# Windowed attention with a gated layer behind it: statistics of the normalisation on ScalarE, one inverse for two softmaxes, shorter scale passes, and a new table of ranks

## Chip, cores and metric

One core of one Trainium2 chip. The metric is the time of one execution in device microseconds (us); the kernel before takes 561.51 us (median of 3 runs, 561.41 to 562.19).

## What is computed

For 8 batches of 8 heads, 576 positions and 64 dimensions: attention within a band of |i - j| < 4, plus attention on means of groups of 4 positions, whose result is repeated 4 times. The sum x goes through a gated layer. The lines that the change touches are the two softmaxes and the normalisation of v:

```python
a = np.exp(s); a = a / (np.sum(a, axis=-1, keepdims=True) + 1e-09)      # both attentions
h = np.maximum(x @ w_in, 0.0)
u, v = h[..., :512], h[..., 512:]
mu = np.mean(v, axis=-1, keepdims=True)
var = np.mean((v - mu) ** 2, axis=-1, keepdims=True)
v_n = (v - mu) / np.sqrt(var + 1e-06)
v_s = np.einsum('ts,bsd->btd', w_spatial, v_n) + b_spatial[None, :, None]
return (u * v_s) @ w_out
```

## The kernel before

Everything runs on one core with five queues: PE (TensorE), DVE (VectorE), ACT (ScalarE), POOL (GpSimd) and SP (DMA issue). The function `tile_kernel` describes the work as some 1,500 pieces (`plan.op`), each with an engine, a cost in ns, the tiles that it reads and writes, and a rank. `Plan.run` then walks through time and gives each engine, among the pieces that can start within `NEAR` of the earliest, the one of lowest rank. The ranks are the table `ORDER`, found by a search, one number per piece in the order in which they are declared. The strings `ON` say, piece by piece, which engine does a step that several could do (A is ACT, D is DVE, P is POOL). So the table and the strings set the order in each queue; waits are by semaphores. Where the planner expects PE to idle in the first 110 us, it puts in dummy matmuls (`warm`, L1341).

The attention runs over 32 pairs of heads (n, four per batch; `attention`). PE makes the banded scores into a PSUM tile paa or pab (L883 mask, L890), DVE takes maxima and subtracts (L903 to L918), ACT takes exponentials (L954), DVE sums (L921) and inverts (L924, L925), DVE or POOL normalises (L958), PE transposes (L966). The attention on means goes the same way: scores L937 into two of the four PSUM tiles pma to pmd, maxima L940 to L942, exponentials with their sums on ACT (L974), inverse L978 and L979, normalisation L989 or L991, for batches from 1 on a rest in half precision (L995). Then PE multiplies by v (L1091 and L1061 or L1075) and DVE adds both results into x (L1101, L1103). In batches from 1 on, x is split into two half-precision parts (L1124, L1126).

The gated layer of a batch (`gated`) has five V pieces of up to 128 rows (PE L1160, L1164, L1169; relu on ACT L1182, L1185 or L1193), eight U pieces (L1226 or L1231, relu L1237 on ACT, with sums that bound the magnitude), eight S pieces (the spatial product, L1253 to L1256, on v normalised and split into two halves vh), and O pieces (L1290, drained by ACT L1303). For each V piece, `stats` on DVE (L1173, L1174, L1176) gives mean and scaled variance, POOL raises it to -1/2 (L1195), DVE applies both (L1179), ACT makes the high half (L1199; L1205 and L1206 for the last 64 rows), DVE or POOL the low half (L1201, L1207).

Weights come as 64-bit floats; DVE unpacks them in `low`, `body` and `sign` (L643, L654, L658), `shrink` (L648, L650) is on either engine; ACT sums magnitudes (L741, L745), and `split` makes two half-precision parts (ACT L616, DVE L619). `bound` turns sums of magnitudes into a power of two and its inverse: a transpose on PE (L586), a maximum on DVE (L589), a spread on PE (L592), and five small DVE passes in `scales` (L597 to L603).

SP issues the loads of q and k (L854), v (L792, L794), and weights (L628), and the stores (L1294, L1300); POOL issues accumulating loads of v for the group means (L780).

## Time and profile before

| | |
|---|---|
| runs | 561.41, 561.51, 562.19 us |
| profiled execution: its own time, its span | 562.08 us, 560.3 us |
| PE busy | 532.8 us, 95% |
| DVE busy | 457.3 us, 82% |
| ACT busy | 355.5 us, 63% |
| POOL busy | 147.3 us, 26% |
| granted TensorE clock, mean | 0.989 |

The span runs from the first to the last instruction; the execution's own time is 1.78 us longer. Starts are counted from the span's beginning. A line's mean duration holds neither the wait before it nor the overlap with its neighbour.

### The profile page before, as it was taken

The numbers are of one execution on the slowest core, as the hardware profiler recorded it, in microseconds if no ns is written. First come the engines' busy times: TensorE is split into PE (matmuls) and PEld (weight loads), VectorE is DVE, ScalarE is ACT, GpSimd is POOL, SyncE is SP. The second block draws the span as 40 slices with busy tenths as digits, with TensorE's granted clock in tenths as the row PEclk, the third lists the DMA queues.
The fourth block names the chain that finished last, engine by engine and source line by source line (L and its number), as shares of the span: only waits on it lengthen the run. The fifth ranks groups of instructions, "written<-read, shape, count | busy, mean of one in ns | idle before, by whom it ended". The sixth has DMA issues, their size and how long they took to land.

```text
span 560.3 us, 15981 instructions
## 1 busy us (share of the span) xinstructions
PE 532.8 (95%) x6457; PEld 357.1 (64%) x6457; DVE 457.3 (82%) x1251; ACT 355.5 (63%) x905; POOL 147.3 (26%) x173
## 2 busy tenths in 40 slices
PE   5668979999999999999999999999999999999997
PEld 3446456865777566865777656856676567856673
DVE  5799999998998699897989798997779897963450
ACT  4759669857976586556766767666546566654422
POOL 6424273102622144011500144111610031111400
PEclk9889999999999999999999999999999999999999
DMA  9997775025441345234431345243253310010002
GB/s 258 282 294 212 197 180 124 1 63 176 89 129 42 108 105 133 86 108 130 111 97 54 92 126 128 87 131 87 35 135 101 109 40 26 5 39 1 37 1 94
DMA packets 40230, 59.54 MB, mean 106 GB/s; under 512 B 4028, under 2 KB 26972, under 8 KB 40158
## 3 DMA queue, kind: packets, MB, share of 16 engines
q1 hardware_dynamic: 37854, 51.46, 30.4%
q0 software_dynamic: 2304, 7.08, 7.9%
q8 instruction: 50, 0.82, 0.6%
q14 instruction: 22, 0.18, 0.1%
HBM read 46.57 MB, written 9.44 MB: 100 GB/s over the span
## 4 chain that ended last, share of the span: by engine, by line
PE 73%; DVE 14%; DMA 6%; ACT 2%; POOL 1%; issue 1%; SPq 1%; ACTq 0%; DVEq 0%; POOLq 0%
PE pmb L1290 6%; PE pma L1253 4%; PE pmd L1253 4%; PE pma L1290 4%; PE pmc L1253 4%; PE pmd L1290 3%; PE pmd L1164 3%; PE pma L1164 3%; PE pma L1231 3%; PE pmb L1253 3%; PE pmc L1231 3%; PE pmc L1290 3%; PE pmd L1231 3%; PE pmb L1164 3%; PE pmb L1231 2%; PE pmc L1164 2%
## 5 line engine op out<-in xcount | busy, mean ns | idle before, releaser
L1253 PEld LDWEIGHTS <-vha 128*128 128x128 f16 x768 | 73.2, 98 | 19.1
L1231 PEld LDWEIGHTS <-win 128*128 128x128 f16 x672 | 65.1, 98 | 17.8 <-issue 0.2
L958 POOL TENSOR_TENSOR sb<-sb,smb 128x640 f32<-128x640 f32 x11 | 15.1, 1374 | 75.4 <-DVE smb L925 45.6
L1290 PEld LDWEIGHTS <-g 128*128 128x128 f16 x192 | 18.5, 98 | 20.8
L1290 PEld LDWEIGHTS <-more 128*128 128x128 f16 x192 | 18.3, 98 | 20.7
L1253 PE MATMUL pma<-wsp,vha 128*128 128x256 f16 (+1 forms) x216 | 28.5, 281 | 0.0
L1253 PE MATMUL pmd<-wsp,vha 128*128 128x320 f16 (+1 forms) x192 | 27.8, 294 | 0.0
L1253 PE MATMUL pmc<-wsp,vha 128*128 128x256 f16 (+1 forms) x204 | 27.0, 282 | 0.0
L1290 PE MATMUL pmb<-wo,more 128*128 128x512 f16 x96 | 22.0, 379 | 0.0
L1253 PE MATMUL pmb<-wsp,vha 128*128 128x320 f16 (+1 forms) x156 | 21.5, 287 | 0.0
L861 POOL TENSOR_TENSOR suma<-qka 128x576 f32<-128x576 f32 x9 | 10.8, 1198 | 37.3 <-DMA qka<-qk_dram 27.5
L958 POOL TENSOR_TENSOR sa<-sa,sma 128x640 f32<-128x640 f32 x8 | 11.1, 1389 | 34.5 <-DVE sma L925 23.3
L1195 POOL TENSOR_TENSOR stc<-stc,mhalf 128x1 f32<-128x1 f32 x13 | 9.0, 691 | 40.8 <-DVE stc L1176 40.8
L1195 POOL TENSOR_TENSOR sta<-sta,mhalf 128x1 f32<-128x1 f32 (+1 forms) x14 | 11.1, 792 | 32.3 <-DVE sta L1176 20.3
L1195 POOL TENSOR_TENSOR stb<-stb,mhalf 128x1 f32<-128x1 f32 (+1 forms) x13 | 9.2, 708 | 36.5 <-DVE stb L1176 32.8
L861 POOL TENSOR_TENSOR suma<-qkb 128x576 f32<-128x576 f32 x7 | 8.1, 1160 | 33.8 <-DMA qkb<-qk_dram 33.8
L780 POOL DMA_DIRECT2D tv<-v_dram x15 | 13.6, 910 | 11.7 <-DMA tv<-v_dram 10.6
L995 DVE SCALAR_TENSOR_TENSOR ehb<-edb,smdb,ehb 128x144 f16<-128x144 f32 x42 | 16.2, 450 | 0.0
L954 ACT ACTIVATE sb<-sb 128x640 f32<-128x640 f32 x16 | 11.7, 732 | 4.8 <-DVE sb L909 4.8
L954 ACT ACTIVATE sa<-sa 128x640 f32<-128x640 f32 x16 | 11.8, 736 | 4.7 <-DVE sa L918 2.6
L1164 PEld LDWEIGHTS <-xa 128*128 128x128 f16 x84 | 8.2, 98 | 9.9
L995 DVE SCALAR_TENSOR_TENSOR eha<-eda,smda,eha 128x144 f16<-128x144 f32 x42 | 14.5, 409 | 0.0
(1023 smaller groups left out, 1712.4 us busy)
## 6 DMA issues: line engine op xcount, KB each, us to landing
qka<-qk_dram SPq DMA_DIRECT2D x16, 576.0 KB
qkb<-qk_dram SPq DMA_DIRECT2D x16, 576.0 KB
tv<-v_dram POOLq DMA_DIRECT2D x15, 288.0 KB, 5.1
wst<-v_dram POOLq DMA_DIRECT2D x9, 288.0 KB, 4.6
stg<-w_in_dram SPq DMA_DIRECT2D x5, 512.0 KB
out_dram<-rowc SPq DMA_DIRECT2D x8, 256.0 KB
out_dram<-rowb SPq DMA_DIRECT2D x7, 256.0 KB
out_dram<-rowe SPq DMA_DIRECT2D x7, 256.0 KB
```

Source lines behind the costliest of these rows:

```text
L780: plan.op("POOL", 850, lambda r=r: nc.gpsimd.dma_start(t.ap, v4[b, r], accum_op=ALU.add), w=[t], rank=rank + 2.0 + 0.3 * r, kb=288, name="tv")
L861: side(s1).tensor_tensor(sb.ap.rearrange("p x (g r) -> p x g r", r=2), x[:, :, :, :2], x[:, :, :, 2:], op=ALU.add)
L954: exp_of.append(plan.op("ACT", 637, lambda: nc.scalar.activation(s.ap, s.ap, AF.Exp, scale=1.0 / 8.0), w=[s], rank=R["E"], name="exp"))
L958: plan.op(nm, 0, lambda: side(nm).tensor_tensor(s.ap, s.ap, sm.ap[:, :, None].broadcast_to([P, NW, 64]), op=ALU.mult), r=[sm], w=[s], rank ...
L995: nc.vector.scalar_tensor_tensor(eh.ap[:, a, :, 1], ed.ap[:, a, :], smd.ap[:, a:a + 1], eh.ap[:, a, :, 0], op0=ALU.mult, op1=ALU.subtract)
L1164: nc.tensor.matmul(ps.ap, xs[c].ap[:, i, t * P:(t + 1) * P], win[:, c, j, FF:], start=(c == 0 and (i, j) == (0, 0)), stop=(c == NC - 1 and ...
L1195: plan.op("POOL", 700, lambda: nc.gpsimd.tensor_tensor(st.ap[:r, 8:9], st.ap[:r, 8:9], mhalf[:r], op=ALU.pow), w=[st], rank=rank - EVICT, ...
L1231: nc.tensor.matmul(ps.ap[:, :n], win[:, c, i, ft * P:(ft + 1) * P], xs[c].ap[:, j, HA[h]:HA[h + 1]], start=(c == 0 and (i, j) == (0, 0)), ...
L1253: nc.tensor.matmul(ps.ap[:, :n], vh.ap[:, c, i, fs], wsp[:, c, j, hs], start=(c == 0 and (i, j) == (0, 0)), stop=False)
L1290: nc.tensor.matmul(ps.ap, g.ap[:, c, i, k:k + P] if t < NT else gt.ap[:, c, i], wo[:, c, j, :], start=(c == 0 and (i, j) == (0, 0)), stop= ...
```

## The change

Part 1, normalisation. Relu on ACT now also sums the row (`accum_out`). A small step `mean` makes -sum/512 on one of three engines, ACT makes a second pass (`squares`, a Square with that bias and a sum), POOL makes the scaled variance and its power -1/2 and, where needed, the product with the mean (`root`), and `apply` is on DVE or ACT. Tile st has five buffers in place of three. `stats` is gone.

```diff
-            def stats():
-                nc.vector.bn_stats(st.ap[:r, :6], vr.ap[:r])
-                nc.vector.bn_aggr(st.ap[:r, 6:8], st.ap[:r, :6])
-                nc.vector.tensor_scalar(st.ap[:r, 8:9], st.ap[:r, 7:8], 1.0e-6, 2.0**-20, op0=ALU.add, op1=ALU.mult)
+            def mean():
+                if mu.eng == "ACT":
+                    nc.scalar.mul(st.ap[:r, 1:2], st.ap[:r, :1], -1.0 / FF)
+                else:
+                    side(mu).tensor_scalar(st.ap[:r, 1:2], st.ap[:r, :1], -1.0 / FF, None, op0=ALU.mult)
+            def squares():
+                nc.scalar.activation(junk[:r, :FF], vr.ap[:r], AF.Square, bias=st.ap[:r, 1:2], accum_out=st.ap[:r, 2:3])
+            def root():
+                nc.gpsimd.tensor_scalar(st.ap[:r, 8:9], st.ap[:r, 2:3], 2.0**-20 / FF, 1.0e-6 * 2.0**-20, op0=ALU.mult, op1=ALU.add)
+                nc.gpsimd.tensor_tensor(st.ap[:r, 8:9], st.ap[:r, 8:9], mhalf[:r], op=ALU.pow)
+                if ap.eng == "ACT":
+                    nc.gpsimd.tensor_tensor(st.ap[:r, 9:10], st.ap[:r, 8:9], st.ap[:r, 1:2], op=ALU.mult)
             def apply():
-                nc.vector.tensor_scalar(vr.ap[:r], vr.ap[:r], st.ap[:r, 6:7], st.ap[:r, 8:9], op0=ALU.subtract, op1=ALU.mult)
+                if ap.eng == "ACT":
+                    nc.scalar.activation(vr.ap[:r], vr.ap[:r], AF.Identity, bias=st.ap[:r, 9:10], scale=st.ap[:r, 8:9])
+                else:
+                    nc.vector.tensor_scalar(vr.ap[:r], vr.ap[:r], st.ap[:r, 1:2], st.ap[:r, 8:9], op0=ALU.add, op1=ALU.mult)
```

Part 2, the softmaxes. The sums of both (10 and 3 columns) stand in one tile; two DVE instructions replace four. `times` holds the factors that differ.

```diff
-            nc.vector.tensor_scalar(sm.ap, sm.ap, 1.0e-9, None, op0=ALU.add)
+            nc.vector.scalar_tensor_tensor(sm.ap, sm.ap, 1.0e-9, times[:, 0 if whole else 1], op0=ALU.add, op1=ALU.mult)
             nc.vector.reciprocal(sm.ap, sm.ap)
-        def inverse_d():
-            nc.vector.tensor_scalar(smd.ap, smd.ap, 1.0e-9, 4.0 if whole else 2.0**-8, op0=ALU.add, op1=ALU.mult)
-            nc.vector.reciprocal(smd.ap, smd.ap)
```

The first eight pairs (`solo`) put the scores on means into one PSUM tile, heads side by side, so one maximum replaces two:

```diff
+            if solo:
+                nc.vector.tensor_reduce(mxd.ap, pd[0].ap[:, :3 * G].rearrange("p (a k) -> p a k", a=3), axis=AX.X, op=ALU.max)
+            else:
+                nc.vector.tensor_reduce(mxd.ap[:, :1], down(0), axis=AX.X, op=ALU.max)
...
```

Part 3, bounds. Five small passes become three; four where the bound has a factor. The floor comes from extra columns that POOL sets at the start (ten more memsets there, one of them in place of DVE's L710).

```diff
-                nc.vector.tensor_copy(t()[:, 7:8], pb.ap[:, P:P + 1])
+                nc.vector.tensor_scalar(e, pb.ap[:, P:P + 1].bitcast(I32), 0x7F800000, None, op0=ALU.bitwise_and)
...
-            nc.vector.tensor_scalar(e, e, -1.0, -low * 2.0**23, op0=ALU.mult, op1=ALU.min)
-            nc.vector.tensor_scalar_add(sc, e, (268.0 - up) * 2**23)
-            nc.vector.tensor_scalar(iv, e, -1.0, (up - 14.0 + fac) * 2**23, op0=ALU.mult, op1=ALU.add)
+            nc.vector.tensor_scalar(sc, e, -1.0, (268.0 - up) * 2**23, op0=ALU.mult, op1=ALU.add)
+            nc.vector.tensor_scalar_add(iv, e, (up - 14.0 + fac) * 2**23)
```

Part 4, the order. `ORDER` is a new table, and `ON` has new strings (two are new):

```diff
-ON = {"shrink": "ADAAAADAADAA",
+ON = {"shrink": "ADAAAAAADDAA",
+      "mean": "PDPPDDADADAPDAAAADDAPAAPDADAPDADDDAPPPD",
+      "apply": "DDDAADADAAAAADDDAADADADDAAADAAAAADDADAAA",
-      "norm": "PDPPPPPPPPDPDPDPPPDPDPPDDDDDDDPP",
-      "normd": "PDAAAAAPAAAPDADDPAAAPPDDAPPPDDPA",
-      "vlo": "PPDPDPPDDDDDDDDPDDDDPPPDDPDPDDPDDDDPDPP"}
+      "norm": "PDPPPPPDDDDDPPDPPPPDDDPDPDDDPDDP",
+      "normd": "DDAAAAAAPDADPPAPAPPAPDAAAPAPDDPD",
+      "vlo": "DDDPDDPDPDDPPDDPDPDDPDPDDDDDPDDDPDDDPPD"}
```

On DVE, in the middle of batch 0's V pieces, before: the statistics of the second piece (row tile rowe), splits of the WV weights (win), and the next statistics.

```order
L1173 BN_STATS stb<-rowe 128x6
L1174 BN_AGGR stb<-stb 128x2
L1176 TENSOR_SCALAR stb<-stb 128x1
L619 SCALAR_TENSOR_TENSOR win<-mbd,sw,win 128x512
L619 SCALAR_TENSOR_TENSOR win<-mbc,sw,win 128x512
L589 TENSOR_REDUCE sw<-pmd 4x1
L1179 TENSOR_SCALAR rowe<-rowe,stb 128x512
L1173 BN_STATS stc<-rowb 128x6
```

The same place with the change (the second piece is in rowc; L1206 applies, L1228 makes low halves, L632 splits weights):

```order
L1228 TENSOR_TENSOR vha<-rowa,vha 128x512
L632 SCALAR_TENSOR_TENSOR win<-mbc,sw,win 128x512
L603 TENSOR_REDUCE sw<-pmc 5x1
L632 SCALAR_TENSOR_TENSOR win<-mbb,sw,win 128x512
L1206 TENSOR_SCALAR rowc<-rowc,stb 128x512
L632 SCALAR_TENSOR_TENSOR win<-mbd,sw,win 128x512
L1228 TENSOR_TENSOR vha<-rowc,vha 128x512
L632 SCALAR_TENSOR_TENSOR win<-mba,sw,win 128x512
L1206 TENSOR_SCALAR rowb<-rowb,stc 128x512
```

The statistics have left DVE; low halves that POOL made stand there, and more splits of weights come in this stretch.

On ACT, in the last batch, before: the end of the V chain (L1199, L1205, L1206 make high halves; rowc is the last 64 rows) between relus of U pieces (L1237).

```order
L1237 ACTIVATE ub,utb<-pmc,sx2a 128x320
L1237 ACTIVATE uf,utb<-pma,sx2a 128x320
L1199 CAST vha<-rowa 128x512
L1205 CAST vta<-rowc 64x512
L1206 CAST vt_106<-rowc 64x512
L1237 ACTIVATE uc,utb<-pmd,sx2a 128x320
L1237 ACTIVATE uh,utb<-pmb,sx2a 128x320
```

The same place with the change: the copy of half the last rows (L1217), their relu (L1220), Square (L1194) and apply (L1204) of the last two pieces (rowa, rowb), and the high halves (L1226, L1233, L1232).

```order
L1217 COPY rowe<-pmc 64x512
L1204 ACTIVATE rowa<-rowa,stc 128x512
L1220 ACTIVATE rowb,ste<-rowe,sx2a 64x512
L1226 CAST vha<-rowa 128x512
L1264 ACTIVATE ui,utb<-pmd,sx2a 128x320
L1194 ACTIVATE junk,ste<-rowb,ste 64x512
L1264 ACTIVATE uh,utb<-pmb,sx2a 128x256
L1264 ACTIVATE ud,utb<-pma,sx2a 128x320
L1204 ACTIVATE rowb<-rowb,ste 64x512
L1233 CAST vt_106<-rowb 64x512
L1264 ACTIVATE uc,utb<-pmc,sx2a 128x320
L1232 CAST vta<-rowb 64x512
```

The V piece of the last 64 rows now comes last of the five on PE, where it came second, and five U pieces and one O piece follow it before the first S piece.

## Rows read from the trace of the kernel before

**Rows 1.** Page, part 1: busy us, share of the span, instructions, of each engine.

```profile
PE 532.8 (95%) x6457; PEld 357.1 (64%) x6457; DVE 457.3 (82%) x1251; ACT 355.5 (63%) x905; POOL 147.3 (26%) x173
```

**Rows 2.** Busy time by stretch: length, PE, PEld, DVE, ACT, POOL, clock, DMA share, GB/s.

```profile
0.00:26.00 26.00, 15.31 (x238) 10.18 (x239) 16.40 (x42) 15.29 (x38) 14.93 (x37) 0.93 1.01 266
26.00:52.60 26.60, 19.91 (x365) 14.27 (x365) 25.87 (x58) 19.40 (x60) 10.40 (x11) 0.87 0.88 255
52.60:84.00 31.40, 27.46 (x221) 14.46 (x220) 30.37 (x87) 21.69 (x58) 13.53 (x15) 1.00 0.78 198
84.00:98.40 14.40, 14.05 (x116) 10.05 (x114) 13.99 (x40) 14.30 (x39) 5.04 (x5) 1.00 0.51 121
98.40:549.40 451.00, 449.17 (x5491) 305.19 (x5491) 370.68 (x1029) 282.74 (x713) 103.38 (x108) 1.00 0.30 82
```

**Rows 3.** Timeline of PE: start, us, instruction, times, idle before it and its releaser.

```profile
52.62 1.02 PE L1160 MATMUL pmb<-mba,xa 128*128 128x512 f32 x2
...
82.61 0.21 PE L1028 MATMUL pma<-ident,eha 112*128 112x112 f16 x1 [1.34 <-ACT eda L974]
...
98.44 1.48 PE L1253 MATMUL pma<-wsp,vha 128*128 128x256 f16 x12
```

**Rows 4.** Timeline of DVE, first statistics and apply of batch 0.

```profile
61.16 0.68 DVE L1173 BATCH_NORM_STATS2 sta<-rowc 128x6 f32<-128x512 f32 x1
...
62.16 0.68 DVE L658 SCALAR_TENSOR_TENSOR mbf<-rowa,mbf 128x512 int32<-128x512 int32 x1
...
67.23 0.54 DVE L1179 TENSOR_SCALAR rowc<-rowc,sta 128x512 f32<-128x512 f32 x1
```

**Rows 5.** Timeline of DVE: maxima, inverses, scale passes; then splits and low halves.

```profile
30.17 0.30 DVE L940 TENSOR_REDUCE mxda<-pmb 128x1 f32<-128x144 f32 x1
...
30.87 0.17 DVE L942 TENSOR_SCALAR mxda<-mxda 128x3 f32<-128x3 f32 x1
...
33.62 0.11 DVE L978 TENSOR_SCALAR smda<-smda 128x3 f32<-128x3 f32 x1
...
33.85 0.79 DVE L921 TENSOR_REDUCE smb<-sb 128x10 f32<-128x640 f32 x1
...
65.22 0.14 DVE L597 COPY sxa<-pmd 128x1 f32<-128x1 f32 x1
...
65.90 0.68 DVE L654 SCALAR_TENSOR_TENSOR mbh<-rowa,mbh 128x512 int32<-128x512 int32 x1
...
70.66 0.74 DVE L619 SCALAR_TENSOR_TENSOR win<-mbc,sw,win 128x512 f16<-128x512 f32 x1
...
83.61 0.68 DVE L1201 TENSOR_TENSOR vha<-rowb,vha 128x512 f16<-128x512 f32 x1
```

**Rows 6.** Timeline of ACT: an accumulator's read-out, a pass with a scale per row.

```profile
67.94 0.19 ACT L745 ACTIVATION_READ_ACCUMULATOR junk<-mbh 128x1 f32 x1
68.03 0.58 ACT L1182 ACTIVATE rowe<-pmb 128x512 f32<-128x512 f32 x1
68.51 0.71 ACT L616 ACTIVATE win<-mbd,sw 128x512 f16<-128x512 f32 x1
69.12 0.71 ACT L616 ACTIVATE win<-mbc,sw 128x512 f16<-128x512 f32 x1
```

**Rows 7.** Timeline of POOL: the first power, then a low half of v.

```profile
62.32 0.94 POOL L1195 TENSOR_TENSOR sta<-sta,mhalf 128x1 f32<-128x1 f32 x1 [4.29 <-DVE sta L1176]
...
79.77 1.47 POOL L1201 TENSOR_TENSOR vha<-rowd,vha 128x512 f16<-128x512 f32 x1
```

**Rows 8.** Chain of waits, PE's U pieces: start, us, what.

```profile
146.22 1.31 PE pmd L1231 x12
...
151.49 1.42 PE pmd L1231 x12
152.91 1.63 PE pma L1231 x12
```

**Rows 9.** Timeline of DVE: three elements per row, beside POOL's work.

```profile
79.42 1.85 DVE L942 TENSOR_SCALAR mxda<-mxda 128x3 f32<-128x3 f32 x1
```

More of the change, by code (lines that the diff above doesn't have):

```diff
@@ L561, in tile_kernel @@
     junk = const.tile([P, NW * D], BF16, name="junk")
+    times = const.tile([P, 2, NW + 3], F32, name="times")
+    nc.gpsimd.memset(times[:, :, :NW], 1.0)
+    nc.gpsimd.memset(times[:, 0, NW:], 4.0)
+    nc.gpsimd.memset(times[:, 1, NW:], 2.0**-8)
     sw = const.tile([P, 4, 16], F32, name="sw")
+    for i, k in enumerate((NC, NC, NT + 2, NF)):
+        nc.gpsimd.memset(sw[:, i, k:k + 1], 2.0**-77)
+    for t in plan.places["sx"]:
+        nc.gpsimd.memset(t[:, NP:NP + 1], 2.0**-97)
+    nc.gpsimd.memset(vt2[TAIL:TAIL + 2], 1024.0)
     near = const.tile([P, P], BF16, name="near")
@@ L576, in side, with bound @@
         return {"DVE": nc.vector, "POOL": nc.gpsimd, "ACT": nc.scalar}[way.eng]
-    def bound(t, k, toks, tok, rank, up, fac, low, times=None, then=None, more=(), also=()):
+    def bound(t, n, toks, tok, rank, up, fac, times=None, then=None, more=(), also=(), at=7):
         pb = plan.buf("pm")
+        k = n if times is not None else n + 1
         def turn_b():
@@ L608, in bound @@
         known = plan.op("PE", 110, spread, r=[tok], w=[pb], rank=rank, lag=PEL, mode="F", name="spread")
-        plan.op("DVE", 1231 if then else 692, scales, r=[pb, *more], w=[tok, *also], rank=rank - EVICT, port=True, name="scale")
+        plan.op("DVE", 960 if then else 420, scales, r=[pb, *more], w=[tok, *also], rank=rank - EVICT, port=True, name="scale")
         return known
@@ L709, in b3 @@
                                            tb.ap[rows, :S], op0=ALU.mult, op1=ALU.add)
-            nc.vector.memset(vt2[rows], 1024.0)
         plan.op("ACT", 1368, b1, r=[tok], w=[tb, ("junk",)], rank=rank, name="bh")
         plan.op("POOL", 300, b2, w=[("sel",)], rank=rank, name="sel")
-        plan.op("DVE", 1300, b3, r=[tb, ("sel",), ("junk",)], w=[("lb", 1), ("one",)], after=wide, rank=rank, port=True, name="lb")
+        plan.op("DVE", 690, b3, r=[tb, ("sel",), ("junk",)], w=[("lb", 1), ("one",)], after=wide, rank=rank, port=True, name="lb")
         return [("hh",), ("lb", 0), ("lb", 1), ("one",)]
@@ L1192, in v_piece @@
                         r=[ps], w=[tmp], rank=rank - EVICT, name="vadd")
-                plan.op("ACT", 626, lambda: nc.scalar.activation(vr.ap[:r], tmp.ap[:r], AF.Relu, scale=iv.ap[:r, :1]), r=[tmp, iv.sub(0)], w=[vr], rank=rank, name="relu")
-            plan.op("DVE", 1006, stats, r=[vr], w=[st], rank=rank, name="stats")
-            plan.op("POOL", 700, lambda: nc.gpsimd.tensor_tensor(st.ap[:r, 8:9], st.ap[:r, 8:9], mhalf[:r], op=ALU.pow),
-                    w=[st], rank=rank - EVICT, name="rstd")
-            plan.op("DVE", 453, apply, r=[st], w=[vr], rank=rank, port=True, name="apply")
+                plan.op("ACT", 676, lambda: nc.scalar.activation(vr.ap[:r], tmp.ap[:r], AF.Relu, scale=iv.ap[:r, :1], accum_out=st.ap[:r, :1]), r=[tmp, iv.sub(0)], w=[vr, st], rank=rank, name="relu")
+            plan.op(mu, 0, mean, w=[st], rank=rank - EVICT, name="mean")
+            plan.op("ACT", 640, squares, r=[vr], w=[st], rank=rank - EVICT, name="square")
+            plan.op("POOL", 900, root, w=[st], rank=rank - EVICT, name="rstd")
+            plan.op(ap, 0, apply, r=[st], w=[vr], rank=rank, name="apply")
             if t < NT:
```

95 lines of the change are left out of this document (48 added, 47 removed), and 285 rows, old and new, of the table ORDER.

## The prediction

> **What bounds the kernel now.** The page's first part says PE, 95% busy [rows 1]; where is answered by busy time by stretch [rows 2]. From 98.4 to 549.4 us PE works 449.17 of 451.00 us, so 1.83 us is all that other engines can return there. Before 98.4 it idles 26.00 - 15.31 = 10.7, then 6.7, then 31.40 - 27.46 = 3.9, then 0.35 us. The first two stretches also hold dummy matmuls, and the DMA engines are 101% and 88% busy, so much of that idle time belongs to loads. DVE is the full engine from 26 to 98.4: 25.87 of 26.60, 30.37 of 31.40, 13.99 of 14.40 us. ACT has 9.7 us free from 52.6 to 84 and 0.1 us from 84 to 98.4.
>
> The timeline of PE gives the marks [rows 3]: the first V piece of batch 0 starts at 52.62, its first S piece at 98.44. Between them lie 45.8 us with 4.3 us of idle time; one wait of 1.34 us there is for ACT. From the S piece on PE runs through. A change pays if that piece starts earlier, and costs if a later PE piece waits.
>
> **The change, part by part.** Durations are spaced start to start. *Statistics leave DVE.* From the first one's start to the next instruction is 1.00 us [rows 4]; five before the first S piece make 5.0. Two of five applies go to ACT: 2 x 0.5 = 1.0. Two means come to DVE; the nearest rows are the small scale passes (0.68/5 = 0.14) [rows 5], so 0.3. The other 35 pieces free 35 us of DVE under a busy PE, which is worth nothing except in the 1.83 us.
>
> *Inverses.* The two instructions that go take 33.85 - 33.62 = 0.23 us [rows 5], times seven pairs before the S piece: 1.6. The wider first inverse costs the same. The normalisation of the bands now waits for the exponentials on means as well; both are issued well ahead, so I take nothing, with the later wait as part of the upper bound.
>
> *Maxima of the first eight pairs.* Two take 30.87 - 30.17 = 0.70 us; the new one has 432 columns, 640 take 0.79 [rows 5]. By columns that is 0.53, so it saves 0.17, 1.2 us for seven (bounds: loss 0.1 to gain 0.4 each). PE pays for putting both heads' scores in fewer quarters of the array; that is early, beside loads.
>
> *Scales.* Five passes take 65.90 - 65.22 = 0.68 us [rows 5]; three take about 3/5, so 0.27 each, and one bound comes after the mark instead of before it: 4 x 0.27 + 0.68 = 1.8.
>
> *What comes in.* The new order puts before the mark four more splits of weights (0.74 each), two more low halves (0.68, formerly POOL's), one more normalisation and one more sum of q and k (both 0.6 by the 0.68 of a two-input pass of 512 columns): 3.0 + 1.4 + 1.2 = 5.6 [rows 5].
>
> DVE up to the first S piece: -(5.0 + 1.0 + 1.6 + 1.2 + 1.8) + 0.3 + 5.6 = -4.7 us. Of this about 1 us lies before the first V piece: four inverses (0.9), six maxima (1.0), a scale and a memset (about 0.7), less one split, one unpacking pass and one normalisation (about 1.7).
>
> *ACT.* Five squares and five longer relus come. The nearest pass is L616 with a scale per row, 69.12 - 68.51 = 0.61, and each read-out of an accumulator adds 68.03 - 67.94 = 0.09 [rows 6]. So 5 x 0.70 + 5 x 0.09 + 2 applies x 0.61 + 2 splits x 0.61 = 6.4; three sums of magnitudes (0.7 each) move behind the last U relu: net +4.3 us in a stretch with 9.8 us free, all but 0.1 of it before 84. An apply takes two columns as operands where L616 has one: bounds 0.61 and twice that. The Trainium skill (ScalarE: Activation LUTs, What ACT_TABLE_LOAD costs) gives about 93 ns for each such operand; by that an apply would be 0.70 and the sum 0.2 us more.
>
> *POOL.* Ten memsets are new at the start and precede POOL's first sum; PE waits for that chain there. I bound their cost from 0 to 1 us (no row stands for the 512-element one) and take 0.5. Each later chain has one or two POOL instructions more beside the power of 0.94 us [rows 7], bounds 0.1 to 0.94 each, taken as 0.2.
>
> *Order on PE.* The same matmuls remain (three more dummies, early). Where another kind of work breaks in, the next U piece takes 1.42 instead of 1.31 us [rows 8]. The new order has 71 such breaks against 79: 8 x 0.11 = 0.9 us.
>
> **The sum.** (a) Until the first V piece: -1 us of DVE, +0.5 of POOL, and loads that hardly move: -0.7, bounds -2.5 and +2. (b) From there to the first S piece: DVE gives 3.7, PE could take 4.3, but ACT must place 4.3 us before 84 and is full after; I take -1.8, somewhat under half, bounds -4.3 and +2.5. (c) After: -0.9 for breaks, +0.4 for waits in new places, -0.5; bounds -2.7 and +5. Together -3.0 against the profiled execution's 562.08 us, so 559.1; the median of the runs is 0.57 lower, so **558.5 us**. A measurement of this kernel tells about 0.2%, 1.1 us, from no change.
>
> The last batch is the tightest of the new waits, since after the last V piece only five U pieces (1.31 + 4 x 1.63 [rows 8]), an O piece (12 matmuls of 512 columns, twice 1.31) and the first twelve S matmuls (1.48 [rows 3]) stand before its result is read: 11.9 us. The chain behind it is a copy 0.58, an addition 0.68, relu 0.58, mean 0.14, square 0.70, POOL 0.94 + 0.4, apply 0.61, two high halves 1.2, low half 1.47: 7.3 us, with some 0.1 per hand-over and three U relus of 0.58 between, 9.9. It fits with 2 us to spare.
>
> **Rivals.** *DVE was the whole bound* (0.18). PE's 4.3 us of idle time and 1.2 us before it are all recovered: 561.5 - 5.5 - 0.9 = 555.1 us. For it: DVE above 96% over 72 us. Against it: ACT's full last stretch, and PE's 1.34 us wait for ACT [rows 3].
>
> *Loads and the order give it back* (0.12). If arrival of weights sets the first stretches, and freed DVE time goes to the splits now ahead, the front stays, breaks and new waits cancel: 561.2 us. DMA at 88% to 101% until 52.6 speaks for it, 78% and 51% after it against.
>
> *POOL holds DVE up* (0.07). A DVE pass over three elements took 1.85 us where its twin takes 0.17, and ended within 0.05 us of a POOL pass beside it (79.42 + 1.85 against 79.77 + 1.47) [rows 5, 7, 9]. The change adds some ten small POOL instructions in batch 0's chains; if each holds DVE for 0.2 us, 2 us of its saving go: 560.5 us. The Trainium skill (SBUF — State Buffer, SBUF: two separate sides) states this as an exclusive lock on the port pair that the two engines share, held for a whole instruction. This row agrees; DVE's loss of statistics makes it matter less.
>
> *ACT takes DVE's place* (0.21), the slower side. A V piece now passes ACT three or four times. If the 4.3 us can't be placed before 84, the last U relus and the low halves end up to 4.3 us later than 98.4, and PE waits for the bound; with -0.7 before and -0.9 after, 561.5 + 4.3 - 1.6 = 564.2 us. It decides when less than half of ACT's 9.7 free us is usable, for a square can't start before its relu. In later batches each chain that ends after its cover adds as much as it is late. The Trainium skill (ScalarE: Activation LUTs, Rules for kernel authors) speaks against the move: relu, add and mul belong on VectorE. The rows agree on the price, 0.54 for an apply on DVE against 0.71 for the like on ACT [rows 4, 6]. By the rule the kernel would lose; by the rows it matters only where ACT is full.
>
> **Chances and range.** The forecast (557 to 560.3) has 0.42, the full recovery 0.18, the two small cases 0.19, ACT's case 0.21. Faster by over 0.2%: 0.42 + 0.18 + half of the POOL case = 0.63. Within 0.2%: the loads case and what is left of POOL's, 0.15. Slower: 0.22 with rounding. The range leaves out a tenth on either side: 554.5 at full recovery with a further 0.6 us, 564.5 at ACT's case.
>
> **What would show it.** DVE's busy time should fall from 457 to about 400 us, ACT's rise to about 400. The first V piece should start between 51 and 53, the first S piece between 94 and 97.5, and PE idle after it stay near 1.8 us. The forecast is wrong if the S piece starts at or after 98.4 (then ACT's stretch before it should be full, and PE's waits name ACT), or if PE's waits after it sum to over 4 us. Recovery in full shows as an S piece before 93.5. POOL's case shows as small DVE passes of over 1 us beside POOL's new instructions.

## The result and the profile after

The kernel with the change takes 566.66 us (median of 5 runs, 566.24 to 569.48), the kernel before beside it 562.19 us (5 runs, 561.41 to 563.69): a ratio of 1.0089, 95% interval 1.0059 to 1.0118. It is slower by about 0.9%. 558.5 us was forecast, in a range up to 564.5 us.

First the engines' totals, from the first part of the page of the kernel after (busy us, share of the span, instructions); its span is 564.9 us, its own time 566.66 us.

```profile
PE 535.0 (95%) x6460; PEld 359.4 (64%) x6460; DVE 403.0 (71%) x1005; ACT 404.4 (72%) x1064; POOL 163.3 (29%) x256
```

Against [rows 1] the change did what it says: 54 us have left DVE, 49 us have come to ACT. PE's busy time rose by 2.2 us, and the span by 4.6.

The marks of [rows 3] in the timeline of PE, after: the first V piece, the first S piece, and the start of the last O piece.

```profile
56.58 0.59 PE L1172 MATMUL pmc<-mba,xa 128*128 128x512 f32 x1
...
99.53 1.16 PE L1280 MATMUL pmd<-wsp,vha 128*128 128x256 f16 x9
...
557.87 1.46 PE L1317 MATMUL pmc<-wo,more 128*128 128x512 f16 x6
```

Busy time by stretch between these marks, kernel after (length, PE, PEld, DVE, ACT, POOL, clock, DMA share, GB/s), with the two stretches of [rows 2] on which ACT's case rested:

```profile
0.00:56.58 56.58, 36.59 (x608) 26.25 (x609) 42.55 (x88) 36.55 (x101) 25.42 (x56) 0.91 0.87 256
56.58:99.53 42.95, 41.33 (x334) 24.68 (x332) 40.06 (x91) 38.42 (x104) 19.93 (x28) 1.00 0.65 166
99.53:557.87 458.34, 454.32 (x5512) 307.39 (x5509) 320.38 (x828) 328.07 (x858) 117.92 (x173) 1.00 0.29 82
...
52.60:84.00 31.40, 29.32 (x245) 16.86 (x242) 28.86 (x70) 28.96 (x75) 16.08 (x24) 1.00 0.72 187
84.00:98.40 14.40, 13.81 (x135) 9.70 (x134) 14.11 (x29) 12.94 (x40) 6.18 (x7) 1.00 0.60 164
```

The same three stretches of the kernel before, by its own marks (its last O piece starts at 553.58):

```profile
0.00:52.62 52.62, 35.25 (x604) 24.45 (x604) 42.29 (x99) 34.71 (x97) 25.35 (x47) 0.90 0.94 261
52.62:98.44 45.82, 41.53 (x335) 24.54 (x334) 44.38 (x126) 36.02 (x96) 18.59 (x20) 1.00 0.70 173
98.44:553.58 455.14, 453.31 (x5510) 307.03 (x5510) 370.64 (x1029) 283.39 (x713) 103.34 (x108) 1.00 0.30 82
```

The 4.6 us come from three places of both signs. The first V piece is 3.96 us late; from there to the first S piece 2.87 us are gained; from the S piece to the last O piece 3.20 us are lost, and 0.3 in the tail behind it. In the first stretch DVE works as long as before (42.55 against 42.29) and idles 14.0 instead of 10.3 us. In the third it works 50 us less, and PE idles 4.02 instead of 1.83 us; PE's busy time there is 1.0 us longer, which holds waits inside pieces as well as work that crossed the mark (nine more turns of the on-means softmax and one more bound, but twelve fewer scores on means), and isn't taken apart here.

What PE waits for after the first S piece, in the two kernels' views of waits (us in total, times, longest), first after, then before:

```profile
PE pma L1258 <- ACT eda L975: 0.7, 1, 0.7
PE pma L1258 <- DVE rowe L1218: 0.6, 1, 0.6
PE pmc L606 <- DVE utc L603: 0.5, 1, 0.5
PE pmd L606 <- DVE uta L603: 0.5, 1, 0.5
PE pmc L606 <- DVE utb L603: 0.4, 1, 0.4
PE pma L606 <- DVE utb L603: 0.4, 1, 0.4
PE pmb L606 <- DVE utb L603: 0.3, 1, 0.3
PE pab L990 <- DVE sb L982: 0.2, 1, 0.2
PE pmb L1258 <- ACT pdTa L1046: 0.2, 1, 0.2
```

```profile
PE paa L966 <- DVE sa L958: 1.2, 1, 1.2
PE pmd L592 <- DVE uta L589: 0.3, 1, 0.3
PE pma L586 <- ACT ud L1237: 0.2, 1, 0.2
```

They sum to 3.8 us after, 1.7 before. Five of the nine waits after are of one kind: the spread of the U bound (L606) stands right behind its transpose (L600), with only a maximum on DVE between them, 2.1 us in all. Of the others one is for an exponential (L975), one for the addition of the two halves of a V piece's last rows (L1218), one for a normalisation (L982).

Last the front. In the timeline of PE the turn of a softmax comes at 41.11 us after an idle time, and the granted clock is 0.50, of the two levels the 1.2 GHz one, already from 40.0 us on, while PE still idles; the same eight matmuls (L1073) take 1.24 us there and 0.72 five us later. The last row is the stretch's, from the view of busy time.

```profile
41.11 1.30 PE L990 MATMUL paa<-ident,sa 128*128 128x128 f32 x5 [3.17 <-DVE xa L1115]
42.34 1.24 PE L1073 MATMUL pab<-pdTa,tv 72*64 72x144 f32 x8
...
47.23 0.72 PE L1073 MATMUL pab<-pdTa,tv 72*64 72x144 f32 x8
```

```profile
41.10:46.60 5.50, 5.49 (x69) 4.41 (x71) 4.10 (x11) 4.87 (x17) 0.84 (x1) 0.50 0.25 83
```

DVE waits on the results of this (its timeline, kernel after):

```profile
44.06 0.71 DVE L1113 TENSOR_TENSOR xb<-pab,dnb 128x232 f32<-128x232 f32 x2 [0.33 <-ACT dnb L1125]
...
46.40 0.82 DVE L923 TENSOR_REDUCE mxa<-paa 128x10 f32<-128x640 f32 x1 [0.79 <-PE paa L901]
...
49.15 0.71 DVE L1113 TENSOR_TENSOR xc<-pab,dna 128x232 f32<-128x232 f32 x2 [0.93 <-ACT dna L1125]
```

So three suspects stood for the front: the half clock (though the kernel before has stretches of it too, and its mean clock up to the V piece is 0.90 against 0.91), POOL's ten memsets (its first sum starts at 5.96 instead of 4.95 us), and two splits of W_sp (0.81 us each) that the new order puts on DVE ahead of the second sum into x.

### The profile page after: what moved, and what is told of

It is laid out like the page before. It is cut to its first block, busy times and chain, and to the rows that moved or that the text cites. A ratio compares the mean times of both kernels' runs of the same rounds, so it can differ in the third digit from the quotient of the medians.

```text
span 564.9 us, 15953 instructions
## 1 busy us (share of the span) xinstructions
PE 535.0 (95%) x6460; PEld 359.4 (64%) x6460; DVE 403.0 (71%) x1005; ACT 404.4 (72%) x1064; POOL 163.3 (29%) x256
## 4 chain that ended last, share of the span: by engine, by line
PE 75%; DVE 12%; ACT 5%; issue 2%; POOL 2%; DMA 1%; SPq 1%; POOLq 0%; ACTq 0%; DVEq 0%
PE pmb L1317 5%; PE pmb L1280 5%; PE pmd L1280 4%; PE pmc L1317 4%; PE pmc L1280 4%; PE pma L1280 4%; PE pmb L1176 4%; PE pmb L1258 4%; PE pmd L1317 3%; PE pma L1317 3%; PE pmd L1176 3%; PE pma L1258 3%; PE pmc L1258 3%; PE pma L1176 3%; PE pmd L1258 3%
## 5 line engine op out<-in xcount | busy, mean ns | idle before, releaser
L1280 PE MATMUL pmb<-wsp,vha 128*128 128x256 f16 (+1 forms) x216 | 28.5, 282 | 0.0
L1280 PE MATMUL pmc<-wsp,vha 128*128 128x320 f16 (+1 forms) x180 | 24.7, 287 | 0.0
L982 POOL TENSOR_TENSOR sb<-sb,sma 128x640 f32<-128x640 f32 x7 | 9.8, 1393 | 38.5 <-DVE sma L936 24.9
L1010 DVE SCALAR_TENSOR_TENSOR eha<-eda,sma,eha 128x144 f16<-128x144 f32 x42 | 16.9, 466 | 3.4 <-POOL eha L1006 2.9
L1010 DVE SCALAR_TENSOR_TENSOR ehb<-edb,smb,ehb 128x144 f16<-128x144 f32 x42 | 16.9, 465 | 3.0 <-POOL ehb L1006 3.0
L914 DVE TENSOR_TENSOR sb<-paa,mask 128x384 f32<-128x384 f32 (+1 forms) x20 | 8.9, 485 | 13.3 <-PE paa L901 13.3
L1317 PE MATMUL pmc<-wo,g 128*128 128x512 f16 x72 | 16.5, 379 | 0.0
L1317 PE MATMUL pmb<-wo,g 128*128 128x512 f16 x60 | 13.8, 379 | 0.0
L1317 PE MATMUL pmc<-wo,more 128*128 128x512 f16 x60 | 13.8, 379 | 0.0
L1006 POOL TENSOR_TENSOR eha<-eda,sma 128x432 f16<-128x432 f32 x5 | 5.3, 1051 | 29.3 <-DVE sma L936 29.3
L914 DVE TENSOR_TENSOR sa<-pab,mask 128x384 f32<-128x384 f32 (+1 forms) x12 | 5.3, 485 | 11.3 <-PE pab L901 11.2
```

What stands on the lines that cost most here:

```text
L914: nc.vector.tensor_tensor(sv, pv, mask[:, None, None, :].broadcast_to(list(pv.shape)), op=ALU.add)
L982: plan.op(nm, 0, lambda: side(nm).tensor_tensor(s.ap, s.ap, sm.ap[:, :NW, None].broadcast_to([P, NW, 64]), op=ALU.mult), r=[sm], w=[s], ra ...
L1006: side(nd).tensor_tensor(to, ed.ap, sm.ap[:, NW:, None].broadcast_to([P, 3, G]), op=ALU.mult)
L1010: nc.vector.scalar_tensor_tensor(eh.ap[:, a, :, 1], ed.ap[:, a, :], sm.ap[:, NW + a:NW + a + 1], eh.ap[:, a, :, 0], op0=ALU.mult, op1=ALU. ...
L1280: nc.tensor.matmul(ps.ap[:, :n], vh.ap[:, c, i, fs], wsp[:, c, j, hs], start=(c == 0 and (i, j) == (0, 0)), stop=False)
L1317: nc.tensor.matmul(ps.ap, g.ap[:, c, i, k:k + P] if t < NT else gt.ap[:, c, i], wo[:, c, j, :], start=(c == 0 and (i, j) == (0, 0)), stop= ...
```

## The experiments

All kernels of this section replay an order: in place of ranks, `Plan.run` takes the pieces from a list `SEQ` in turn, and the dummies from a table `DUMMIES` by position. Every edit of the order is then an edit of that list alone, and nothing else moves. Each ran beside the kernel before on the same chip; medians of 5 or more runs, the ratio with its 95% interval.

### Code and order, crossed

The new code in the order of before (steps that only the new code has stand where their forerunners stood), and the old code in the new order:

```diff
-ORDER = [  # new code, its own ranks
+SEQ = [    # new code, the old order, old ON strings; means on POOL, applies on DVE
-ORDER = [  # old code, its own ranks
+SEQ = [    # old code, the new order, new ON strings
```

> The changed code (statistics on ScalarE, one inverse, three-pass scales), with its pieces issued in the order of the kernel before: same total order, same choice of engines and the same dummy matmuls; all forty means on GpSimd right behind the relu, the squares where the old statistics stood, all applies on VectorE, st with twelve free buffers so that no new buffer binds. If the new order is what lost the time (theory one), this comes out at or below the kernel before, 558 to 561.5. If the new instructions themselves cost it (theory two), it stays at 565 or more. If each code needs an order searched for it (theory three), it too lies above 565, and so does its mirror image.

> The code of before, with its pieces issued in the changed kernel's order (same total order, engines and dummies; the old statistics where the squares stand, the second inverse right behind the first). Theory one (the order lost it): slower than before by as much as the changed kernel or more, 566 to 572, with the first V piece at 56 us or later. Theory two (the new instructions lost it): about 562 or less. Theory three (each code needs its own order): well above 566, because VectorE's 55 us of old work stand in an order that counts on their absence.

Measured: 593.49 us (590.62 to 595.33), ratio 1.0576 [1.0546, 1.0606]; and 590.69 us (586.91 to 594.10), ratio 1.0521 [1.0483, 1.0559]; before beside them 562.27. The four corners are thus 562, 593, 591 and 567 us: each order fits only its own code. Without a new order the new code would have cost 31 us, so the search won back some 27 of them. The change's price can't be put on the code alone or on the order alone.

### The half clock

```diff
-DUMMIES = {31: 1, 50: 6, 90: 2, 104: 6, 123: 7}
+DUMMIES = {31: 1, 50: 6, 90: 2, 104: 6, 123: 7, 138: 12}
```

> The changed kernel with twelve more dummy matmuls in the 3.2 us in which TensorE idles before the turn of sa at 41.1 us, nothing else. If the half granted clock of 40 to 47 us is what delays the first V piece (theory clock), that stretch is granted 1.0, its pieces go back to 0.7 to 0.8 us each, the first V piece starts at 53.5 to 54.5 us and the time falls by 2 to 3 us, to 563.5 to 564.5. If VectorE's chain or the loads set the first V piece (theory queue), the granted clock rises but the V piece stays within 0.7 us of 56.6, and the time at 566 to 567.

Measured: 565.86 us (565.08 to 567.82), ratio 1.0078 [1.0054, 1.0102]. The clock still fell, and was at 0.50 from 43 to 49 us: twelve dummies, which ended 2.04 us ahead of the turn, didn't hold it. Then the gaps were filled in five places, with the kernel before so treated as a control:

```diff
-DUMMIES = {31: 1, 50: 6, 90: 2, 104: 6, 123: 7}
+DUMMIES = {31: 1, 50: 15, 67: 7, 90: 8, 104: 14, 123: 7, 138: 14}
```

> The changed kernel with dummy matmuls in all five gaps of TensorE over 1.5 us before the first V piece (9, 7, 6, 8 and 14 more, some 0.21 us each at full clock), nothing else. Theory clock: no stretch of half granted clock is left between 16 and 56 us, or it lies where TensorE is not waited for; the values that now run from 42.3 to 47.9 us take 4 us again, the first V piece starts at 53 to 54.5 us and the time falls to 563 to 564.5. Theory queue (VectorE's chain and the loads set the first V piece): granted clock 1.0 throughout, and the first V piece at 56 us or later all the same. If filling one gap only shifts the half clock to the next, the clock stays at 0.5 somewhere in 40 to 48 us and the runs scatter; then the clock can't be bought this way.

> A control: the kernel before, with dummies in its gaps over 1.5 us ahead of the turn of sa at 40.6 us (13, 9, 10 and 9 more). There TensorE's half-clock stretches lie at 16 to 19, 26 to 29 and 33 to 36 us, none on the chain to the first V piece, which is VectorE's. Theory clock: no gain, 561.5 to 562.5, because the clock is not waited for there. If it gains 1 us or more, the clock costs the kernel before as well, and is no special loss of the change.

Measured: 565.41 us (562.45 to 568.74, 12 runs), ratio 1.0079 [1.0053, 1.0104]; the control 563.68 us, ratio 1.0032 [1.0009, 1.0056]. In the profiled execution the clock now held throughout, and the marks came early (V piece 54.39, S piece 96.88):

```profile
0.00:54.39 54.39, 43.09 (x652) 28.11 (x653) 42.98 (x88) 36.41 (x101) 25.67 (x56) 1.00 0.98 266
```

Yet the median is within a measurement of the change's own (1.0079 against 1.0089). So in the profiles the V piece comes earlier without the half clock, but the clock is not what makes the kernel slower. The control only lost (its V piece stands at 56.12 in its profile, 3.5 us later than without the dummies); why was not taken apart.

### The memsets and the splits

```diff
-    nc.gpsimd.memset(times[:, :, :NW], 1.0)
...
+    def later():                            # the ten memsets, behind POOL's first sum and key sum
+        nc.gpsimd.memset(times[:, :, :NW], 1.0)
...
```

> The changed kernel with its ten new memsets on GpSimd issued behind the first pair's two sums instead of ahead of them, nothing else. If the chain to the first V piece begins with GpSimd's constants (theory head), the first sum goes back from 5.96 to about 4.95 us, the first score on means follows, and the first V piece and the end move by 0.5 to 1.0 us: 565.7 to 566.2. If a later link (the loads, VectorE, the clock) takes the microsecond up, the first sum moves and the first V piece stays within 0.4 us, the time at 566.3 to 567.

> Both edits together: the memsets behind the first sums and the dummies in all five gaps. Theory clock and theory head both right: the two gains add, first V piece at 52 to 53.5 us, time 562 to 563.5, level with the kernel before. If VectorE's chain sets the first V piece, no more than 1 us below the changed kernel.

Measured: 567.24 us, ratio 1.0107 [1.0071, 1.0142]; with the dummies as well 566.02 us (562.46 to 568.53, 12 runs), ratio 1.0075 [1.0050, 1.0100]. PE's first wait for POOL was back at 1.18 us in the first, from 2.05 (1.07 in the kernel before), and nothing came of it at the end. With the dummies as well, the profiled execution was the fastest of the 12, 562.46 us, and its marks are the earliest of all (view of busy time):

```profile
0.00:51.91 51.91, 41.23 (x653) 27.69 (x653) 40.41 (x88) 36.97 (x101) 26.13 (x56) 1.00 1.01 277
51.91:94.88 42.97, 41.33 (x334) 24.67 (x333) 40.05 (x91) 38.41 (x104) 20.12 (x28) 1.00 0.68 169
```

In that execution the front is regained in full: the V piece is 0.7 us and the S piece 3.6 us earlier than in the kernel before. What keeps it from being faster lies behind the S piece, where it takes 465.7 us against 461.9. Why the other executions of this kernel take up to 6 us longer isn't known, since only one was profiled. Then the two splits of W_sp were moved behind the fourth sum into x, alone and together with both other edits:

```diff
 SEQ: DVE, ahead of the second sum into x
-L632 SCALAR_TENSOR_TENSOR wsp<-wst,sw,wsp
-L632 SCALAR_TENSOR_TENSOR wsp<-wst,sw,wsp
 SEQ: DVE, behind the fourth
+L632 SCALAR_TENSOR_TENSOR wsp<-wst,sw,wsp
+L632 SCALAR_TENSOR_TENSOR wsp<-wst,sw,wsp
```

> The changed kernel with the two low halves of W_sp, which VectorE splits between the first and the second sum of attention planes (41.5 and 42.9 us, 0.81 us each), put behind the fourth; nothing else in any engine's order, though the two buffers of the on-means values trade places. Theory queue (VectorE's chain xa, xb, xc, xd sets the first V piece, and the new order put 1.5 us of other work into it): the first V piece 1.0 to 1.5 us earlier, the time 565.0 to 565.8. If TensorE at half clock is what VectorE waits for there, the second plane comes early, the third waits longer, and the time stays at 566.2 to 567.

> All three edits of the stretch before the first V piece together: GpSimd's memsets behind the first sums, dummies in TensorE's five gaps, the two splits of W_sp behind the fourth plane. If these three are what delays the first V piece by 4 us, it starts at 50.5 to 54 us and the time is 562 to 564; what is left above the kernel before would be the 0.7 us that the rest of the program costs. If it stays above 565, the first V piece is set by something not yet named, such as the loads.

Measured: 569.05 us, ratio 1.0132 [1.0099, 1.0165], with DVE idle for 1.60 us where the splits had stood; and 566.72 us (565.27 to 568.78), ratio 1.0099 [1.0071, 1.0128]. In the view of busy time of the kernel with all three edits:

```profile
0.00:52.72 52.72, 41.28 (x653) 27.67 (x653) 40.22 (x87) 37.02 (x102) 23.91 (x54) 1.00 0.97 265
52.72:98.42 45.70, 41.62 (x335) 24.56 (x333) 43.23 (x92) 38.61 (x104) 22.75 (x29) 1.00 0.65 169
```

The V piece stands at 52.72, where the kernel before has it; by the profile above, the clock and the memsets are enough for that, without the splits. But the S piece stands at 98.42, as before as well: the stretch between them is 2.75 us longer than in the changed kernel, nearly all of it idle time of PE (45.70 - 41.62 = 4.08 against 1.62). Its waits there:

```profile
PE pmc L607 <- ACT junk L764: 1.6, 2, 1.4
PE paa L997 <- POOL sb L989: 1.3, 1, 1.3
PE pma L607 <- ACT uh L1271: 0.7, 1, 0.7
```

These are sums of magnitudes of later weights, a normalisation and U relus. The early V piece isn't the reason: in the six kernels that have the new code and order and leave the splits in place, this stretch is 42.5 to 43.0 us, with V pieces from 51.91 to 58.00. It is longer only in the two that move the splits, 43.96 and 45.70, and the wait for the normalisation is found only there. So moving the splits gave nothing ahead of the V piece (56.62 against 56.58 alone, 52.72 against 51.91 with the others), and a longer stretch behind it.

### The spread of the U bound

Each spread that stood right ahead of an S piece was moved behind it, and the rule that such a piece follows the spread was dropped:

```diff
-hold=[g, u], after=[known], rank
+hold=[g, u], rank
 SEQ: PE
-L606 spread of the U bound
 L1280 S piece
+L606 spread of the U bound
```

> The changed kernel with the spread of the U bound (one matmul that waits for VectorE's maximum over the turned bound) put behind the first S piece that follows it instead of in front, in the batches where turn and spread stood next to each other; the rest of the order is the same, though PSUM buffers get other numbers. If TensorE's waits for that maximum (0.37, 0.51, 0.51, 0.37 us in the changed kernel's trace) are real losses of the stretch that TensorE bounds (theory waits), the time falls by 1.4 to 2.0 us, to 564.7 to 565.3. If another wait takes their place at once, because the gates then run late (theory shift), it stays within 0.6 us of 566.7.

Measured: 568.24 us (567.78 to 569.84), ratio 1.0121 [1.0098, 1.0145]. Of the five waits one is left, and PE's waits sum to 4.5 us against 3.8, elsewhere (view of waits after the first S piece):

```profile
PE paa L990 <- POOL sb L982: 1.0, 1, 1.0
PE pmb L1040 <- DVE ehb L1010: 0.7, 1, 0.7
PE pma L1258 <- ACT eda L975: 0.7, 1, 0.7
PE pmb L1040 <- DVE eha L1010: 0.6, 1, 0.6
PE pmb L1258 <- DVE rowe L1218: 0.6, 1, 0.6
```

So removing these waits gains nothing. In the eight kernels up to here with the new code and the new order, one profile each, the way from the S piece to the span's end is 465.0 to 466.7 us, whatever was done in front; in the old code in its order it is 461.8 and 461.9.

### The parts, one by one, in the old order

Old code and old order, with one part of the change after the other. First part 3 alone, the scales in three passes, with its six constants set by POOL behind its first sums; then the same with the constants set by DVE at the start:

```diff
-            nc.vector.tensor_scalar_add(sc, e, (268.0 - up) * 2**23)
-            nc.vector.tensor_scalar(iv, e, -1.0, (up - 14.0 + fac) * 2**23, op0=ALU.mult, op1=ALU.add)
+            nc.vector.tensor_scalar(sc, e, -1.0, (268.0 - up) * 2**23, op0=ALU.mult, op1=ALU.add)
+            nc.vector.tensor_scalar_add(iv, e, (up - 14.0 + fac) * 2**23)
...
```

> The kernel before with one part of the change alone: the scales of the bounds in three small passes instead of five (and one pass instead of two for the products of each batch), its order kept piece for piece, the small constants written by GpSimd behind the first pair's sums. Theory one (VectorE's saved time reaches the end wherever VectorE is full, 26 to 84 us): 44 fewer VectorE instructions of 0.09 to 0.18 us, some 1 us of them before the first S piece, so 560.5 to 561.5 against 561.6 to 562.2. Theory three (an order searched for other durations loses what is saved): 562 or more.

> The kernel before with the three-pass scales alone, its six small constants written by VectorE in the 2.9 us in which it waits for the first scores, GpSimd's order as before. before_scales had the stretch behind the first S piece at 460.5 us against 461.9 and the one ahead of it at 44.5 against 45.8, but its first V piece came 1.1 us late. If GpSimd's memsets between the first sums did that, 558.5 to 560.5, faster than both kernels; if it was the scatter of the loads, 560.5 to 561.5, level with the kernel before.

Measured: 560.87 us (559.28 to 565.75, 12 runs), ratio 1.0008 [0.9983, 1.0033]; and 561.03 us (12 runs), ratio 0.9991 [0.9970, 1.0013]. No change that can be told, though DVE's busy time fell by 6 us, and the way from S to the end is 460.5 and 461.0 us. Next to it the joint inverse:

```diff
-            nc.vector.tensor_scalar(sm.ap, sm.ap, 1.0e-9, None, op0=ALU.add)
+            nc.vector.scalar_tensor_tensor(sm.ap, sm.ap, 1.0e-9, times[:, 0 if whole else 1], op0=ALU.add, op1=ALU.mult)
...
-        def inverse_d():
```

> The kernel before with two parts of the change, the three-pass scales and one inverse per pair for both softmaxes, in the old order; the pieces that need the inverse wait for it where the order had them earlier. Theory one: another 64 VectorE instructions fewer, 559.5 to 561. Theory three: the scaling of the on-means softmax now waits for the local one's row sum, TensorE's turns wait for it, and the time is 564 or more; then the inverse is the part that makes the old order unfit. If it stays within 1 us of the kernel before, the statistics on ScalarE alone made the 31 us that the whole changed code lost in the old order.

Measured: 582.93 us (581.17 to 584.49), ratio 1.0382 [1.0352, 1.0411], 22 us over the scales alone beside it. PE's waits after the first S piece (L1035 is the transpose of the on-means softmax, L606 the spread):

```profile
PE pma L1035 <- DVE eha L1001: 1.7, 1, 1.7
PE pmc L1035 <- POOL eha L1001: 1.5, 1, 1.5
PE pmb L1035 <- DVE ehb L1005: 0.9, 1, 0.9
PE pab L985 <- DVE sb L977: 0.9, 1, 0.9
PE pmd L1035 <- DVE ehb L1005: 0.8, 1, 0.8
```

These are the largest; in all the transposes wait 6.7 us in nine places, and the same 234 of them are 4.5 us longer where a wait falls inside a piece (this line's PE time after the S piece, before and with the joint inverse):

```profile
98.44:553.58 455.14, 16.55 (x234) 14.08 (x234) 1.00 0.30 82
```

```profile
103.15:575.00 471.85, 21.08 (x234) 14.66 (x234) 1.00 0.29 79
```

The old order put the normalisation of the on-means softmax ahead of the band's row sum. With one inverse for both it must wait for that sum, and on PE the transposes behind it wait too. These two figures are 11.2 of the 15.7 us by which the way from the S piece to the end is longer than with the scales alone (476.2 against 460.5). Last the statistics on ACT, beside the scales:

```diff
-            def stats():
+            def mean(): ...      # on POOL
+            def squares(): ...   # on ACT
+            def root(): ...      # on POOL
+            def apply(): ...     # on DVE
```

> The kernel before with the three-pass scales and the normalisation's statistics on ScalarE (means on GpSimd, applies on VectorE, twelve statistics buffers), two inverses per pair as before, and the old order piece for piece. Theory inverse: the statistics alone do no harm in the old order, 559 to 562.5, the stretch behind the first S piece 460 to 462.5 us. If the statistics' longer chain (mean on GpSimd, square on ScalarE, root on GpSimd) is what costs, 565 to 572 with TensorE waiting for S pieces' inputs or for ScalarE; the whole changed code in the old order took 593 and the inverse with the scales 583, so up to 10 us are to be explained.

Measured: 569.04 us (566.76 to 570.22), ratio 1.0124 [1.0101, 1.0147]. In the view of waits DVE now stands still for POOL's power, ahead of the applies (22 waits, 46.8 us by the line's own row); the three largest groups by tile:

```profile
DVE rowd L1205 <- POOL stall L1197: 16.6, 4, 10.5
DVE rowe L1205 <- POOL stall L1197: 13.7, 6, 3.0
DVE rowc L1205 <- POOL stall L1197: 6.9, 4, 4.7
```

DVE works 29 us less than with the scales alone (422.4 against 451.3), gives the time up in waits, and the stretch from V to S grows from 44.54 to 48.84 us, and the way from S to the end from 460.5 to 464.9. Against 1.0008 for the scales, the statistics cost 1.2%, some 6.5 us, and the inverse 3.7%, some 21. With the scales' zero that makes 27 to 28 of the 31 that all parts cost in the old order; the joint maximum of the first eight pairs was not tried alone.

### Two inverses in the new order

Does the joint inverse also cost in the order that was searched for it? The changed kernel with an inverse for each softmax, the second at the place of the one; and, beside it, the same with that inverse and the normalisation on means moved up to where their data is ready, with and without the spread's move:

```diff
-            nc.vector.scalar_tensor_tensor(sm.ap, sm.ap, 1.0e-9, times[:, 0 if whole else 1], op0=ALU.add, op1=ALU.mult)
+            nc.vector.tensor_scalar(sm.ap, sm.ap, 1.0e-9, None, op0=ALU.add)
...
+        def inverse_d():
+            nc.vector.tensor_scalar(smd.ap, smd.ap, 1.0e-9, 4.0 if whole else 2.0**-8, op0=ALU.add, op1=ALU.mult)
+            nc.vector.reciprocal(smd.ap, smd.ap)
```

> The changed kernel with two inverses per pair again, both at the place of the one, and no other piece moved. Theory moves (it was moving small pieces up in engines that take their work strictly in turn that cost after_two_inverses its 35 us): 565.5 to 568.5, the stretch behind the first S piece 465 to 466.5 us. Theory inverse (the new order still pays for the joint inverse): below 565. If it is above 580, taking the inverse apart costs by itself, and the joint inverse is a gain in the new order.

> The changed kernel with the softmaxes' inverse taken apart again: the on-means one has its own two small passes right behind its exponentials, and its scaling and remainder move up to where their inputs are then ready; everything else keeps its order. Theory inverse (the one inverse ties the on-means chain to the local row sum, some 4 us later, and TensorE's turns of it come late): TensorE's turns of the on-means exponentials lose their hidden waits (13.5 us for 244 of them, 12.6 for 236 before), the stretch behind the first S piece falls from 465.4 to 463.5 to 464.5 us, and the time to 564 to 566. Theory order (only the places of turn and spread cost there): that stretch stays within 0.5 us of 465.4.

> The same with the spread of the U bound behind the next S piece, as in after_spread, where the four waits went away and turns of the on-means exponentials waited 1.3 us instead. Theory inverse: with the chain decoupled nothing takes the waits' place, and the stretch behind the first S piece is 461.5 to 463 us, the time 562 to 564.5. If it is 465 or more, the new order has no slack anywhere, and neither part by itself is the cause.

Measured: 573.05 us, ratio 1.0200 [1.0171, 1.0230]; moved up 601.07 us, ratio 1.0715 [1.0683, 1.0748]; with the spread's move 603.61 us, ratio 1.0741 [1.0712, 1.0771]. The two with moves fail as tests: in queues that run in order, the steps pulled ahead hold up others, and PE's waits for the band's normalisation (L990 behind L982) alone come to 14 us after the first S piece in the kernel of 601.07 us. The first says that in the new order one inverse is worth some 6 us against two. But like the crosses it puts code into an order that was searched for other code, so it tells what the joint inverse is worth in this order, and not what an order searched for two would take. It gives no sign that the joint inverse is by itself the reason for the 4.5 us.

## Why the prediction was wrong

**The bound.** Right: from the first S piece on PE is the bound, and 50 us less of DVE's work are worth nothing there. The control is the kernel with the scales alone, where 6 us of DVE's time went at no change.

**Step (a), until the first V piece: -0.7 forecast, +3.96 in the profile.** This failed most in size, and lies outside its own bound of +2. Its named terms, -1 and +0.5, make -0.5; for the other -0.2 it gives no source. Where the step took 1 us off DVE before this mark, DVE worked 0.3 us longer (passes that run beside POOL's among it), and idled 3.7 us more. The memsets were priced at 0.5 within 0 to 1 and moved POOL's first sum by 1.01. The step had no term for a stretch of half clock: in the eight profiles of the new code in the new order the V piece starts at 56.6 to 58.0 in the five with gaps of PE left unfilled, and at 51.9 to 54.4 in the three with all of them filled. It counted one more split by its busy time, but not that two now stand ahead of the second sum into x; no run shows that this costs. Without the half clock and the memsets' delay the marks came back, and one execution took 562.46 us, yet the medians stayed at 565.4 to 566.7. So this term is not the one that decides, and how large it is in most executions stays open.

**Step (b), from V to S: -1.8 forecast, -2.87 in the profile.** Right in sign and kind. DVE's work up to the S piece fell by 82.61 - 86.67 = -4.1 us (-4.7 forecast), and PE's idle time in the stretch from 4.29 to 1.62. The gain is steady: 42.5 to 43.0 us in six kernels of the new code in the new order, wherever their V piece starts, against 45.82. Taken together (a) and (b) gave +1.1 instead of -2.5; the S piece at 99.53 is on the side named as showing the forecast wrong.

**Step (c), after the S piece: -0.5 forecast, +3.5 in the profile.** This is the step that decides, since the way from the S piece to the end stays at 465.0 to 466.7 us in every replay that leaves the order behind the mark nearly as it is, against 461.8 and 461.9 in the old code and order. The term "+0.4 for waits in new places" was mis-sized: the idle time is 2.2 us longer. And the -0.9 for fewer breaks had thin ground: in the chain of waits of [rows 8] the U piece at 148.07 follows a break as well (a turn of the band's softmax at 147.37) and takes 1.31 us, not 1.42. With 71 breaks in place of 79 the U pieces did not get shorter; the time of their line after the S piece, before and after:

```profile
98.44:553.58 455.14, 85.82 (x672) 65.12 (x672) 1.00 0.30 82
```

```profile
99.53:557.87 458.34, 86.62 (x672) 65.07 (x672) 1.00 0.29 82
```

The waits were mis-sized, as far as the runs tell, because the lengthened chains were costed only in the last batch, and elsewhere only by their busy time. The sentence on inverses, "both are issued well ahead, so I take nothing", looks at the band's normalisation, which now waits for the exponentials on means. It has no term for the other wait, of the on-means normalisation for the band's row sum, and in the order of before that makes the joint inverse cost 21 us; in the new order no run shows such a cost. The statistics' chain, where each further instruction on POOL was priced at 0.2 us, costs 6.5 there, as DVE stands in its queue behind an apply. The search for a new order won nearly all of this back. That the remaining 3.5 us are what the longer chains leave is the reading that fits the parts; it isn't shown, for no order was found for the new code without them, and a longer search might find one.

**The rivals.** *ACT takes DVE's place* had the sign and nearly the size (564.2), by another mechanism, so its nearness is luck. ACT placed its work: from 52.6 to 84 it rose from 21.69 [rows 2] to 28.96 us, and from 84 to 98.4 it fell to 12.94 of 14.40. After the mark PE's waits name ACT for 0.9 us and DVE for the other 2.9. An apply on ACT was priced at 0.61; it is 265.71 to 266.42, 0.71 start to start:

```profile
265.71 0.80 ACT L1204 ACTIVATE rowa<-rowa,stb 128x512 f32<-128x512 f32 x1
266.42 0.19 ACT L1189 ACTIVATE stc<-stc 128x1 f32<-128x1 f32 x1
```

The estimate of 0.70 from the Trainium skill's 93 ns per operand (ScalarE: Activation LUTs, What ACT_TABLE_LOAD costs) agrees with that row. *DVE was the whole bound* fell with the S piece. *POOL holds DVE up* is seen in single places, and no run weighed it. In the timelines of DVE and POOL, after, three columns take 1.20 us beside POOL's sum, where the twin of [rows 5] takes 0.17:

```profile
56.30 1.20 DVE L960 TENSOR_SCALAR mxdb<-mxdb 128x3 f32<-128x3 f32 x1
```

```profile
56.02 1.44 POOL L872 TENSOR_TENSOR suma<-qka 128x576 f32<-128x576 f32 x1
```

Here POOL's pass began 0.28 us before DVE's. In [rows 7, 9] it began 0.35 us after it, so that row shows the common end, but not which engine held up the other.

*Loads and the order give it back* came nearest in kind: in front DVE idles more, and the order's fit is what the crosses measure. It was given 0.12, and only "no change". Whether the loads set the front in the slower executions was not tried.

## What to carry to other kernels

In a kernel whose order was searched, an edit that joins two chains or lengthens one should be costed at every place where the slower part is waited for, not by busy time; replaying the old order with one part of the change at a time gives that price directly, and here it was 21 us for an edit that saves two instructions. Busy time taken from an engine that isn't the bound was worth nothing here: 6 us less of DVE's work with the scales alone left the time as it was. A recorded order that can be replayed also separates code from order: when both crosses lose 5%, the question is how the order fits the code, and not only the price of an instruction. A profile is one execution: compare its time with the median before its marks are taken for those of the kernel.

## What the runs showed of the hardware

- The granted clock was at 0.50, the 1.2 GHz level, from 40.0 us, within 3.17 us in which PE idled, and stayed there until 46.6 although PE was busy for 5.49 of the last 5.50 us. Twelve dummies that ended 2.04 us before the next work didn't prevent it (0.50 from 43 to 49 us); dummies in all gaps did (1.00 up to 54.39).
- One kernel's executions scatter by more than the change's effect: 562.45 to 568.74 us over 12 runs with the gaps filled, and 558.62 to 565.12 over 29 of the kernel before beside it. A single profile of the front therefore settles little: 562.46 us was profiled where the median is 566.02. The part behind the S piece varied less, 465.0 to 466.7 us in eight kernels.
